# Layer norm in smaller groups, activation tables loaded early, copies out of PSUM shared with VectorE, loads and weight folds interleaved: a new prologue for a fused attention and FFN kernel

## The chip, the cores and the metric

The kernel runs on one core of a Trainium2 chip. The metric is the time of one execution in microseconds of device time. The profile's span is some 1.7 us shorter than that time (195.4 for a run of 197.16). Executions of this kernel fall into bands, and the result section tells them apart by span and mean granted TensorE clock. A run more than 1.5% above the fastest of its kernel counts as slow; all others are fast, and ratios use fast runs alone. In the profile, PE is TensorE, PEld its weight loads, DVE is VectorE, ACT is ScalarE and POOL is GpSimd. PSUM is the memory that TensorE writes; its results must be copied out to SBUF, the main on-chip memory.

## The reference

```python
def reference(A_x, A_wqkv, A_w_phi, A_wo, B_x, B_w1, B_w2):   # cut
    xn = layernorm(A_x)                       # [1, 2048, 448], no scale or bias
    q, k, v = split_heads(xn @ A_wqkv)        # 16 heads of 28
    pq, pk = q @ w_phi, k @ w_phi             # per head, 28 x 28
    phi = lambda p: concat(softmax(p), softmax(-p))
    kv = einsum("bhsf,bhsd->bhfd", phi(pk), v); z = phi(pk).sum(over s)
    o  = (phi(pq) @ kv) / (phi(pq) @ z + 1e-6)
    return A_x + o @ A_wo + silu(xn @ B_w1) @ B_w2          # hidden size 1792
```

The attention is linear, with sums over all tokens, so any assignment of tokens to tiles gives the same answer. `w_phi` can be multiplied into the q and k weights once, before the tokens are processed; this is called the fold below. `rstd` below is one over the standard deviation of a token, by which layer norm multiplies.

## The kernel before

A small scheduler collects operations with their reads and writes, adds the semaphore waits and emits them **in program order on each engine**. An engine that waits for one operation therefore does nothing else until it comes. The 2048 tokens are 16 tiles of 128.

```python
# prologue (order of emission; what each part runs on is noted)
def ln_stats(t):     # DVE: bn_stats, bn_aggr -> mean and variance of tile t
def ln_rstd(g, n):   # POOL: add eps, pow(-0.5), for n tiles at once
def ln_apply(t):     # DVE: xn = (x - mean) * rstd, bf16
def xn_transpose(t): # PE: four transposes into PSUM bank "tp"
def xnT_evac(t0):    # DVE: PSUM -> SBUF for a pair of tiles
def emit_wprep_transposes_r(r):   # PE: 8 weight transposes; ACT: copy out of PSUM
    tp_banks = [B_TP, B_PQ[0], B_PQ[1], B_TP]
    ...
def emit_wphi_chain():            # DVE: centre w_phi, block-diagonal form
def emit_wprep_fold():            # PE: wT x w_phi -> wk2, wq2; copies out of PSUM:
    ...                           # ACT, but DVE for q folds 1 and 3
def emit_kv_zero():               # DVE: clear PSUM banks 4, 5

LNG = 4; LA = 6
LF = LA + LNG - 1
for t in range(0, 4): ln_front(t)            # stats; rstd after tile 3
emit_wprep_transposes_r(2); emit_wprep_transposes_r(3)      # k weights
for t in range(0, 4): xn_make(t)             # apply, transpose, copy the pair
emit_wphi_chain(); late_loads()
emit_wprep_transposes_r(0); emit_wprep_transposes_r(1)      # q weights
for t in range(4, 8): ln_front(t)
emit_wprep_fold(); emit_kv_zero()
for t in range(4, LA): xn_make(t)
for t in range(8, LF): ln_front(t)

for t in range(NT):                          # the token loop
    if t + LF < NT: ln_front(t + LF)
    if t + LA < NT: ln_apply(t + LA)
    kv_proj(t); k_exps(t); v_evac(t); k_norm(t)   # PE; ACT; ACT; DVE, DVE, POOL
    q_block(t)                                    # PE, then two exps on ACT
    if t + LA < NT: ...                           # transpose, copy of a pair
    if t >= 1: kv_acc(t - 1)
kv_acc(NT - 1); rhs_build()
# then the long stretch: four FFN blocks, one attention tile, one output tile a round
```

The token loop looks six tiles ahead with normalisation and nine with statistics. x is loaded in four DMAs of four tiles, and each output tile is stored by a DMA of its own.

The softmax here doesn't subtract the row's maximum and nothing guards it: scores larger than these inputs give would overflow.

## Time and profile before

| | before |
|---|---|
| median, all its first 16 runs | 198.73 us (197.15 to 201.41) |
| profiled run | 197.16 us, span 195.4, mean clock 0.991 |
| first key projection | 22.02 us |
| long stretch of TensorE begins | 79.31 us |
| last output addition begins | 192.61 us |

A table of busy time by stretch divides the span. Its columns are the stretch, its length, busy time and instruction count of PE, PEld, DVE, ACT and POOL, then TensorE's granted clock, DMA share and GB/s. These rows cover the prologue, the loop and the long stretch of the kernel before:

```profile
0.00:22.00 22.00, 8.99 (x88) 8.30 (x89) 12.01 (x30) 7.34 (x11) 4.11 (x15) 1.00 0.76 215
22.00:75.00 53.00, 49.08 (x347) 28.92 (x345) 37.70 (x63) 38.57 (x78) 27.85 (x19) 0.97 0.13 38
75.00:178.00 103.00, 100.49 (x637) 51.44 (x636) 51.21 (x123) 43.26 (x67) 2.20 (x2) 1.00 0.04 13
```

Read each row by its fullest engine. In the prologue that is VectorE, busy 12.01 us although nothing reached it before 5.83. TensorE is the fullest engine in the two stretches after that. ScalarE has 14.7 free microseconds in the prologue.

### The profile page before, as it was taken

How to read it: one execution, taken by the hardware profiler on the slowest of the kernel's cores; microseconds unless marked ns; L12 is line 12 of the kernel's file. 1: busy time of each engine (PE TensorE's matmuls, PEld its weight loads, DVE VectorE, ACT ScalarE, POOL GpSimd, SP SyncE). 2: the span in 40 equal slices, each digit the busy share in tenths (PEclk: the TensorE clock that was granted, in tenths of full speed). 3: DMA queues.
4: the chain of work that ended last, by engine and by line, in shares of the span. 5: the costliest groups of instructions: out<-in, count | busy, mean ns of one | idle time of the engine just before them, and what ended most of it. 6: DMA issues, size and time to landing. Idle time of an engine off the chain costs nothing.

```text
span 195.4 us, 2897 instructions
## 1 busy us (share of the span) xinstructions
PE 173.1 (89%) x1152; PEld 96.4 (49%) x1152; DVE 106.7 (55%) x227; ACT 90.2 (46%) x156; POOL 34.2 (17%) x35
## 2 busy tenths in 40 slices
PE   0349696996999995899999999999999999999994
PEld 0338364553655553444545545545545545455551
DVE  0559895995775553377626336336345355288221
ACT  2307366676678888457343433433424424420200
POOL 3111136555556566000000000000000000000000
PEclk9999789999999999999999999999999999999999
DMA  5947980000000000000000000000000000000001
GB/s 159 306 163 196 293 254 1 0 2 5 0 0 3 0 0 2 3 0 0 0 27 0 23 23 0 29 23 0 23 29 0 23 23 3 23 18 29 26 24 47
DMA packets 9022, 8.70 MB, mean 45 GB/s; under 512 B 880, under 2 KB 8560, under 8 KB 9008
## 3 DMA queue, kind: packets, MB, share of 16 engines
q1 hardware_dynamic: 7616, 7.31, 12.7%
q10 hardware_dynamic: 1392, 1.20, 2.2%
q8 instruction: 9, 0.15, 0.3%
q14 instruction: 5, 0.04, 0.1%
HBM read 6.68 MB, written 1.84 MB: 44 GB/s over the span
## 4 chain that ended last, share of the span: by engine, by line
PE 69%; DVE 3%; POOLq 1%; issue 1%; ACT 1%
PE ps L553 25%; PE ps L634 22%; PE ps L637 6%; PE ps L570 3%; PE ps L443 3%; PE ps L510 3%; PE ps L451 2%; PE ps L495 2%; PE ps L612 2%; DVE xn_sb L409 1%; DVE S_sb L475 1%; POOLq L199 1%; ACT E_sb L461 1%; PE ps L422 1%; DVE R_sb L479 0%
## 5 line engine op out<-in xcount | busy, mean ns | idle before, releaser
L559 ACT ACTIVATE hT_sb<-ps 128x512 bf16<-128x512 f32 x56 | 33.4, 597 | 52.8 <-PE ps L553 52.8
L553 PE MATMUL ps<-xnT_sb,w_sb 112*128 112x512 bf16 x224 | 50.7, 379 | 0.0
L634 PE MATMUL ps<-w_sb,hT_sb 128*128 128x448 bf16 x224 | 45.0, 352 | 0.0
L553 PEld LDWEIGHTS ps<-xnT_sb,w_sb 112*128 112x128 bf16 x224 | 19.5, 98 | 27.2 <-ACT hT_sb L559 8.9
L481 POOL TENSOR_TENSOR phik_sb<-E_sb,R_sb 128x896 bf16<-128x896 f32 x16 | 27.6, 1724 | 28.1 <-DVE R_sb L479 23.9
L634 PEld LDWEIGHTS ps<-w_sb,hT_sb 128*128 128x128 bf16 x224 | 21.3, 98 | 17.9
L583 DVE RECIPROCAL rneg_sb<-ps 128x16 f32<-128x16 f32 x16 | 4.1, 256 | 38.1 <-PE ps L570 38.1
L475 DVE TENSOR_REDUCE S_sb<-E_sb 128x32 f32<-128x896 f32 x16 | 17.3, 1082 | 10.5 <-ACT E_sb L461 10.5
L646 DVE TENSOR_TENSOR y_sb<-ps,x_sb 128x448 bf16<-128x448 f32 x16 | 10.0, 625 | 16.9 <-PE ps L637 16.9
L518 ACT ACTIVATE EqT_sb<-ps 112x512 bf16<-112x512 f32 x32 | 17.4, 594 | 3.9 <-PE ps L510 3.9
L510 PE MATMUL ps<-xnT_sb,wq_sb 112*112 112x512 bf16 x64 | 17.0, 389 | 0.0
L422 PE MATMUL ps<-ident_sb,xn_sb 128*112 128x128 bf16 x64 | 7.1, 249 | 9.8 <-DVE xn_sb L409 9.5
L451 PE MATMUL ps<-wv_sb,xnT_sb 112*128 112x448 bf16 x64 | 15.5, 367 | 0.0
L443 PE MATMUL ps<-wk_sb,xnT_sb 112*128 112x448 bf16 x64 | 15.2, 360 | 0.0
L637 PE MATMUL ps<-wo_sb,EqT_sb 112*128 112x448 bf16 x64 | 14.8, 353 | 0.0
L458 ACT ACTIVATE E_sb<-ps 128x448 f32<-128x448 f32 x16 | 8.7, 544 | 12.0 <-PE ps L443 11.7
L409 DVE TENSOR_SCALAR xn_sb<-x_sb,mv_sb,rstd_sb 128x448 bf16<-128x448 bf16 x16 | 10.4, 667 | 5.3 <-POOL rstd_sb L402 5.3
L619 ACT ACTIVATE EqT_sb<-ps 112x1024 bf16<-112x1024 bf16 x8 | 8.2, 1024 | 11.0 <-PE ps L612 10.8
L391 DVE BATCH_NORM_STATS2 stats_sb<-x_sb 128x6 f32<-128x448 bf16 x16 | 9.6, 598 | 5.8 <-DMA x_sb<-in_A_x_dram 5.8
L422 PEld LDWEIGHTS ps<-ident_sb,xn_sb 128*112 128x112 bf16 x64 | 5.6, 149 | 13.9 <-DVE xn_sb L409 13.1
L495 PE MATMUL ps<-vaug_sb,phik_sb 128*112 128x113 bf16 x128 | 9.5, 215 | 2.5 <-POOL phik_sb L481 2.5
L510 PEld LDWEIGHTS ps<-xnT_sb,wq_sb 112*112 112x112 bf16 x64 | 8.7, 136 | 5.6 <-issue 0.8
(49 smaller groups left out, 159.7 us busy)
## 6 DMA issues: line engine op xcount, KB each, us to landing
w_sb<-in_B_w_dram SPq DMA_DIRECT2D x2, 1568.0 KB, 11.2
x_sb<-in_A_x_dram SPq DMA_DIRECT2D x4, 448.0 KB, 8.7
out_dram<-y_sb SPq DMA_DIRECT2D x16, 112.0 KB, 1.7
hT_sb<-in_A_wqkv_dram ACTq DMA_DIRECT2D x2, 392.0 KB, 6.2
wv_sb<-in_A_wqkv_dram ACTq DMA_DIRECT2D x1, 392.0 KB, 8.8
wo_sb<-in_A_wo_dram SPq DMA_DIRECT2D x1, 392.0 KB, 8.9
wphi_sb<-in_A_w_phi_dram SPq DMA_DIRECT2D x1, 24.5 KB, 5.4
```

What stands on the lines that cost most here:

```text
L422: last = e.transpose(out=bank_bf(B_TP)[0:KC, half * 512 + c * P: half * 512 + (c + 1) * P], in_=xn_sb[:, slot, c * KC:(c + 1) * KC], ident ...
L443: last = e.matmul(bank(B_PK[s2])[:, 0:D], lhsT=xnT_sb[:, c, t * P:(t + 1) * P], rhs=wk2_sb[:, c, :], start=(c == 0), stop=(c == NC_ - 1))
L451: last = e.matmul(bank(B_V)[:, 0:D], lhsT=xnT_sb[:, c, t * P:(t + 1) * P], rhs=wv_sb[:, c, :], start=(c == 0), stop=(c == NC_ - 1))
L475: sch.add("dve", lambda e: e.tensor_reduce(out=S_sb[:, s2, :], in_=E_sb[:, s2, :].rearrange("p (g f) -> p g f", f=DH), axis=AX.X, op=ALU.add),
L481: sch.add("pool", lambda e: e.tensor_tensor(out=phik_sb[:, s2, :].rearrange("p (g f) -> p g f", f=DH), in0=E_sb[:, s2, :].rearrange("p (g ...
L495: last = e.matmul(bank(B_KV[sg])[0:KC, j * NV:(j + 1) * NV], lhsT=phik_sb[:, s2, sg * D + j * KC: sg * D + (j + 1) * KC], rhs=vaug_sb[:, s ...
L510: last = e.matmul(bank(B_PQ[slot])[0:KC, :], lhsT=wq2_sb[:, c, j * KC:(j + 1) * KC], rhs=xnT_sb[:, c, tg * TG:(tg + 1) * TG], start=(c == ...
L518: sch.add("act", lambda e, sg=sg: e.activation(out=EqT_sb[:, j, sg, tg * TG:(tg + 1) * TG], in_=bank(B_PQ[slot])[0:KC, :], func=ACTF.Exp, ...
L553: last = e.matmul(bank(B_PQ[slot])[:, :], lhsT=w1_sb[:, c, k * P:(k + 1) * P], rhs=xnT_sb[:, c, tg * TG:(tg + 1) * TG], start=(c == 0), st ...
L559: sch.add("act", lambda e: e.activation(out=hT_sb[:, k, tg * TG:(tg + 1) * TG], in_=bank(B_PQ[slot])[:, :], func=ACTF.Silu), reads=["bank: ...
L634: last = e.matmul(bank(B_ACC[s2])[:, 0:D], lhsT=hT_sb[:, k, t * P:(t + 1) * P], rhs=w2_sb[:, k, :], start=(k == 0), stop=False)
L637: last = e.matmul(bank(B_ACC[s2])[:, 0:D], lhsT=oT_sb[:, c, t * P:(t + 1) * P], rhs=wo_sb[:, c, :], start=False, stop=(c == NC_ - 1))
```

## The change

The intent is to start normalisation after two tiles, not four, to hide ScalarE's table loads, to share PSUM copies between two engines, and to move x and y in longer runs. The diff, cut to its core:

```diff
-    x2 = A_x[0]
-    out2 = out[0]
+    x3 = A_x[0].rearrange("(p t) d -> p t d", t=NT)      # 3584 B runs a load
+    out3 = out[0].rearrange("(p t) d -> p t d", t=NT)
 ...                                                     # loads: wqk0 to the SP queue, x2 to the ACT queue
+        sch.add("act", ... activation(out=dummy_sb[:, 0:1], in_=epsln_sb[:, 0:1], func=ACTF.Sqrt) ...)
 ...  emit_wprep_transposes_r
-                if False:
+                if r % 2 == 1:                          # copy on DVE, else ACT
 ...  emit_wprep_fold -> emit_wprep_fold_qk(qk)
-                    if qk == 1 or i % 2 == 0:           # copy on ACT, else DVE
+                    if i % 2 == 0:
 ...  ln_rstd, path "act":
+                sch.add("act", ... veps = Sqrt(var + eps) ...)
+                sch.add("dve", ... rstd = reciprocal(veps) ...)
 ...  final_out: one store for two tiles
+            if t % 2 == 1:
+                dma("sp", out3[:, t0:t0 + 2, :], y_sb[:, s4 - 1:s4 + 1, :], ...)
 ...
+        groups = [(0, 2, "act"), (2, 4, "act"), (4, 8, "pool"), (8, 12, "pool"), (12, 16, "pool")]
 ...  prologue
+        ln_front(0); ln_front(1)
         emit_wprep_transposes_r(2); emit_wprep_transposes_r(3)
+        ln_apply(0); ln_apply(1); ln_front(2); ln_front(3)
+        ... activation(out=dummy_sb[:, 1:2], ..., func=ACTF.Exp)      # preload
         emit_wphi_chain()
+        xn_transpose(0); xn_transpose(1); xnT_evac(0)
+        emit_wprep_fold_qk(1)
+        ln_apply(2); ln_apply(3); xn_transpose(2); xn_transpose(3); xnT_evac(2)
         late_loads()
         emit_wprep_transposes_r(0); emit_wprep_transposes_r(1)
         for t in range(4, 8): ln_front(t)
+        emit_wprep_fold_qk(0)
         emit_kv_zero(); ...
 ...  loop: q_block(0) in iteration 1
```

## The prediction

> **What bounds the kernel now.** I read the page's slices first, then the chain of waits, then the order of work of VectorE before 23 us, because the change touches only the front of the kernel and its stores.
>
> Two rows of the slices of the page (each digit is the busy tenth of 4.9 us):
>
> ```profile
> PE   0349696996999995899999999999999999999994
> DVE  0559895995775553377626336336345355288221
> ```
>
> From the sixteenth slice on TensorE is full; in the first five it is not, and there VectorE (DVE) is the fuller engine. The chain that ended last says the same (start, length, what):
>
> ```profile
> 78.69 0.62 PE ps L495 x8
> 79.31 3.46 PE ps L553 x16
> ...
> 191.81 0.77 PE ps L637 x4
> 192.58 0.02 issue
> 192.61 0.62 DVE y_sb L646
> ```
>
> In it TensorE alone runs from 79.31 to 192.58 without a gap. So 113 us are matmuls that the change doesn't touch: the change can gain or lose only in the time until the first key projection (L443), in the token loop (to 79 us), and in the tail after the last matmul. The loop's start in TensorE's order of work (start, busy time):
>
> ```profile
> 21.45 0.73 PE L422 MATMUL ps<-ident_sb,xn_sb 128*112 128x128 bf16 x8 [2.01 <-DVE xn_sb L409]
> 22.02 1.37 PE L443 MATMUL ps<-wk_sb,xnT_sb 112*128 112x448 bf16 x4
> ```
>
> TensorE waited 2.01 us for VectorE to normalise tiles 4 and 5. VectorE's order of work up to there (lines of it, start, busy time, idle before and its releaser):
>
> ```profile
> 5.83 0.63 DVE L391 BATCH_NORM_STATS2 stats_sb<-x_sb 128x6 f32<-128x448 bf16 x1 [5.83 <-DMA x_sb<-in_A_x_dram]
> ...
> 10.33 0.70 DVE L409 TENSOR_SCALAR xn_sb<-x_sb,mv_sb,rstd_sb 128x448 bf16<-128x448 bf16 x2 [1.48 <-POOL rstd_sb L402]
> 11.92 0.69 DVE L432 COPY xnT_sb<-ps 112x1024 bf16<-112x1024 bf16 x1 [0.89 <-PE ps L422]
> 12.53 0.69 DVE L409 TENSOR_SCALAR xn_sb<-x_sb,mv_sb,rstd_sb 128x448 bf16<-128x448 bf16 x2
> 14.11 0.69 DVE L432 COPY xnT_sb<-ps 112x1024 bf16<-112x1024 bf16 x1 [0.89 <-PE ps L422]
> ...
> 18.93 1.17 DVE L382 CAST wq_sb<-ps 112x448 bf16<-112x448 f32 x2
> 20.31 0.91 DVE L387 MEMSET ps<- 128x1024 f32 x1 [0.21 <-ACT wq_sb L378]
> 21.13 0.56 DVE L409 TENSOR_SCALAR xn_sb<-x_sb,mv_sb,rstd_sb 128x448 bf16<-128x448 bf16 x2
> ```
>
> From 5.83 to 21.7 VectorE idles only 1.48+0.89+0.89+0.21 = 3.47 us. It is the prologue's bound: what is put onto it, or makes it wait, moves the loop's start. In the loop up to about 55 us it also paces: POOL's products start 3.34 us apart (38.20, 41.55, 44.89), while TensorE's share of a tile is 3.0 us.
>
> **What the Trainium skill says.** "ScalarE: Activation LUTs", section "What ACT_TABLE_LOAD costs": a load takes about 1283 ns and its drain 1380 ns; with a pointer bias an activation costs about 280 ns plus its elements; "Table sets: the hidden batching unit" adds that exp and sqrt lie in different sets, while copy is in every set. The trace agrees with the load (1.28 us at 2.42 and at 76.70) and with copy needing no second load before exp; the drain and sqrt it does not show. "DMA: Bandwidth & Descriptors", section "Queues, rings and completion order": each DMA engine alternates between queues by packets of several descriptors. So a queue with longer descriptors should get more of the engine (my inference); not visible in before, where both queues have 896 B runs. "TensorE: Matmul & The Clock Gate", part 1: matmuls after a few us of idleness run at half clock; the trace agrees (four key matmuls busy 1.37 us at 22.02, 0.92 us later). "SBUF — State Buffer", "Who interferes with whom": VectorE's fast modes and GpSimd lock each other out; the trace agrees (normalising a tile takes 264 ns at least, 1.34 us beside POOL's product at 35.34).
>
> **The change part by part.** Slots below are start-to-start times on VectorE from its order of work: statistics of a tile 0.73, normalisation 0.33, copy of a transposed pair 0.61, weight fold out of PSUM 0.59, phi weights 1.15 (14.71 to 15.86), memset 0.82.
>
> What VectorE loses: the wait for POOL's rstd (1.48). What it gains: two transposed-weight copies from ScalarE (estimate 0.53 each, the 0.61 scaled by 896/1024 elements), two more fold copies (0.59 each), two tiny reciprocals (estimate 0.15 each, from the 0.18 of the small ops). That is 2.5 us more work against 1.5 us of wait. ScalarE, which is relieved, was idle most of the prologue (7.34 busy of the first 22 us).
>
> But engines work in order, so the new order must be walked. The k weights land at 6.2 (TensorE's first transpose is at 6.22) and the 16 weight transposes take 1.75, so to 8.0. Statistics 0, 1 and their sqrt and reciprocal fit before that (5.83+1.46+0.5 = 7.8). VectorE then:
> - copy of transposed weights 3: 8.0 to 8.5; normalise 0, 1 to 9.2; statistics 2, 3 to 10.65; sqrt on ScalarE and reciprocal, about 0.5, to 11.15; phi weights to 12.3; copy of pair 0 to 12.9.
> - folds of k start only at 12.35, a fold takes 0.375 (32 matmul groups of four, 2.99 us for eight): fold 1 is done at 13.1, copied to 13.7; fold 3 at 13.85, copied to 14.45.
> - normalise 2, 3 to 15.1; their transposes end 1.55 after the first normalisation began (10.33 to 11.92 now), at 16.0; copy to 16.65. Idle 0.9.
> - The q weights' transposes use the same PSUM bank, so begin at 16.65 and take 1.71; copy 1 of them is now VectorE's, ahead of the next statistics: idle 1.7, copy 18.35 to 18.9. This is the worst new wait: before, the same transposes ran beside the statistics of tiles 4 to 7.
> - statistics 4 to 7 to 21.8; q fold copies to 23.0; memset to 23.8; normalise 4 starts 23.8 instead of 21.13.
>
> The first key projection follows 0.89 after it, as now: 24.7 instead of 22.02, **+2.7**. In short, from 8.0 on 12.5 us of slots and idle of 0.35 (sqrt), 0.2 and 0.15 (folds), 0.9, 1.7 = 3.3: as much idle as the old 3.47, and the added work comes on top.
>
> Table preloading: sqrt's load (1.28) follows ScalarE's DMA issues, ends about 4, hidden. The exp load after the second sqrt ends at about 12.4 (with a drain 13.7), before or about when the first k fold must be copied by ScalarE: not on the path. Gain 0: exp's load was never on the path (one load at 2.42, hidden).
>
> Query block 0 moved from iteration 0 to 1: same work. Before, VectorE waited 0.24 at 28.27 for the second key exponentials, which stood behind that block; this may go: **-0.25**. Groups 8 to 11 and 12 to 15 stay with POOL, so the stalls of 1.91 and 1.90 us for rstd at 32.94 and 47.94 stay. The VectorE/POOL cycle and the two stalls carry a late start through; I see no slack in which it is regained.
>
> Loads: x goes from runs of 896 B to 3584 B. x arrives sooner, but what starts the chain is the k weights at 6.2, which may lose bandwidth beside the longer runs of x and the q weights now third on the other queue: estimate **+0.2** (between -0.3 and +0.7; x0 plus k weights are 840 KB, 2.8 us at the 306 GB/s of the second slice). Later loads are needed long after landing.
>
> Stores: 16 of 112 KB become 8 of 224 KB. In the loop they are hidden. The last must now carry twice the bytes after the last addition (ends 193.23, span ends 195.4): 112 KB more at 306 GB/s is 0.37, less what longer runs save: **+0.3**.
>
> Sum 2.7-0.25+0.2+0.3 = 2.95, on 197.88: about **200.8 us**, 1.5% slower.
>
> **Rivals.** (1) The intended gain: the LN wait of 1.48 and the waits of 0.89 for transposes vanish behind other work, the loop starts near 19.5, 195.3 us. For it: those waits are truly on the path. Against: VectorE's added 2.5 us, and its in-order waits for folds and q transposes; even with no wait after 8.0 but the second sqrt's (0.35), VectorE's slots sum to 12.5 us and normalise 4 starts at 20.8, only 0.3 earlier than now; 195.3 would need 18.6. (2) Table thrash: if copies between the sqrts need their own set, each switch is 1.28 to 2.66 us and sits before the second sqrt, on VectorE's path: 202 to 204. Against: copy and exp share one load now. (3) The loss is hidden: the loop's first tiles run on a cold clock and with loose coupling, so a later but more complete start (q block later, warmer array) loses only 1 us: 199. For: 4.1 us were spent from 22.02 to 26.08 on the first tile. Against: VectorE's statistics and key sums, not TensorE, lead to the rstd stall at 31.0. (4) Late k weights: up to 1 us more, 201.8.
>
> **Range and chances.** Rival 3 and early weights give the lower end, 198.8; late weights and part of rival 2 the upper, 203.2. Two per cent slower is 201.84, 1 us above my centre: chance 0.23. Two per cent faster is 193.9 and would need the loop to start 4 us sooner, which the slot sum forbids: 0.03. Within 2%: 0.74.
>
> **What would show it.** In the changed profile: first key projection (L443's line moved) at 24 to 25.5 us; VectorE idle 1.5 us or more before the copy of the second q-weight half, waiting for TensorE; VectorE busy 2 us more before that; three table loads; stalls of 1.5 to 2 us for POOL's rstd in the loop still there; TensorE's gapless stretch starting 2 to 3 us later than 79.15; the time from the last addition to the end 0.2 to 0.4 longer. Wrong would be: k weights landing before 5.5, a first projection before 22, extra table loads, or the stalls in the loop shrinking.

## The result, and the profile after

The changed kernel took **202.48 us** (median of 11 runs, 200.64 to 204.41) against 198.73 before (16 runs). The ratio is 1.0179, with a 95% interval of 1.0133 to 1.0224, so it is about 1.8% slower and the interval lies on both sides of two per cent. Two of the 11 runs (203.68 and 204.41) were slow, and two of the 16 (200.50 and 201.41) lie as far above their fastest; the medians include them, the ratio does not. Here and below, a ratio is the mean time of one kernel's fast runs over that of the other's fast runs of the same rounds, so it is not quite the ratio of the medians.

These are the same two slice rows after the change, with the row of granted clock:

```profile
PE   0445399699699999699999999999999999999993
DVE  0674979699495455337564264264264264288321
PEclk9999999999999999799999999999999999999999
```

TensorE's full stretch starts a slice later. The 7 in the clock row at slice 17 is a second, smaller matter, taken up below.

VectorE's order of work in the changed kernel shows the waits (start, busy time, what, then the idle time before it and its releaser):

```profile
7.28 0.17 DVE L420 RECIPROCAL rstd_sb<-veps_sb 128x2 f32<-128x2 f32 x1 [0.36 <-ACT veps_sb L416]
8.34 0.62 DVE L356 COPY hT_sb<-ps 112x896 bf16<-112x896 bf16 x1 [0.90 <-PE ps L346]
...
11.42 0.17 DVE L420 RECIPROCAL rstd_sb<-veps_sb 128x2 f32<-128x2 f32 x1 [0.36 <-ACT veps_sb L416]
...
13.87 1.37 DVE L388 CAST wk_sb<-ps 112x448 bf16<-112x448 f32 x2 [0.55 <-PE ps L372]
...
16.74 0.69 DVE L449 COPY xnT_sb<-ps 112x1024 bf16<-112x1024 bf16 x1 [0.89 <-PE ps L439]
19.32 0.62 DVE L356 COPY hT_sb<-ps 112x896 bf16<-112x896 bf16 x1 [1.89 <-PE ps L346]
...
24.95 0.56 DVE L426 TENSOR_SCALAR xn_sb<-x_sb,mv_sb,rstd_sb 128x448 bf16<-128x448 bf16 x2
```

The wait of 1.48 for POOL's rstd is gone, and two waits of 0.36 for ScalarE's sqrt stand in its place. But two lines are new: copies of transposed weights (L356) now sit on VectorE, behind waits of 0.90 and 1.89 us for TensorE. Tile 4, which gates the loop, is normalised at 24.95 instead of 21.13.

TensorE's order of work shows where this leads:

```profile
25.27 1.10 PE L439 MATMUL ps<-ident_sb,xn_sb 128*112 128x128 bf16 x8 [3.46 <-DVE xn_sb L426]
26.16 1.70 PE L460 MATMUL ps<-wk_sb,xnT_sb 112*128 112x448 bf16 x4
...
37.41 0.43 PE L439 MATMUL ps<-ident_sb,xn_sb 128*112 128x128 bf16 x4 [1.76 <-DVE xn_sb L426]
...
82.36 0.65 PE L512 MATMUL ps<-vaug_sb,phik_sb 128*112 128x113 bf16 x8 [2.17 <-POOL phik_sb L498]
82.83 5.30 PE L570 MATMUL ps<-xnT_sb,w_sb 112*128 112x512 bf16 x16
```

TensorE waits 3.46 us for tile 4 (2.01 before), and the first key projection starts at 26.16. The delay then travels:

| start of | before | after | difference |
|---|---|---|---|
| normalise tile 4 | 21.13 | 24.95 | +3.82 |
| normalise tile 8 | 32.94 | 36.96 | +4.02 |
| normalise tile 12 | 47.94 | 51.96 | +4.02 |
| long stretch | 79.31 | 83.01 | +3.70 |
| second FFN round | 83.19 | 88.55 | +5.36 |
| last output addition | 192.61 | 197.97 | +5.36 |
| end of span | 195.4 | 201.0 | +5.6 |

There are three parts: 3.7 us from the prologue, 1.66 us in the first FFN round, and 0.24 us after the last addition. The 1.66 us are the slice with clock 7. The sixteen FFN matmuls of that round took 5.12 us in the chain, against 3.45 to 3.50 in every later round.

That part does not belong to the change alone. The changed kernel's ten fast runs whose spans are on record (one more than the median counts) have two bands: four from 198.9 to 199.2 at clock 1.0, and six from 200.7 to 201.5 at 0.983 to 0.992. The profiled run is of the longer band, while the profiled run of before is of that kernel's shortest. Shortest band against shortest band (198.9 against 195.3 us in the runs of the experiments) gives 3.6 us; the medians differ by 3.75.

### The profile page after: what moved, and what is told of

It is laid out like the page before. It is cut to its first block, busy times and chain, and to the rows that moved or that the text cites.

```text
span 201.0 us, 2883 instructions
## 1 busy us (share of the span) xinstructions
PE 175.4 (87%) x1152; PEld 97.1 (48%) x1152; DVE 109.3 (54%) x233; ACT 90.4 (45%) x157; POOL 32.9 (16%) x34
## 4 chain that ended last, share of the span: by engine, by line
PE 68%; DVE 3%; POOL 1%; issue 1%; ACT 1%; POOLq 0%
PE ps L570 25%; PE ps L651 21%; PE ps L654 6%; PE ps L587 3%; PE ps L460 3%; PE ps L527 3%; PE ps L468 2%; PE ps L512 2%; PE ps L629 2%; DVE xn_sb L426 1%; DVE S_sb L492 1%; POOL phik_sb L498 1%; ACT E_sb L478 1%; PE ps L439 1%; DVE R_sb L496 0%
## 5 line engine op out<-in xcount | busy, mean ns | idle before, releaser
L570 PE MATMUL ps<-xnT_sb,w_sb 112*128 112x512 bf16 x224 | 52.4, 388 | 0.0
L570 PEld LDWEIGHTS ps<-xnT_sb,w_sb 112*128 112x128 bf16 x224 | 20.0, 100 | 28.4 <-ACT hT_sb L576 8.6
L527 PE MATMUL ps<-xnT_sb,wq_sb 112*112 112x512 bf16 x64 | 16.3, 379 | 0.0
L468 PE MATMUL ps<-wv_sb,xnT_sb 112*128 112x448 bf16 x64 | 15.0, 358 | 0.0
```

The lines of the kernel that those rows point to most:

```text
L468: last = e.matmul(bank(B_V)[:, 0:D], lhsT=xnT_sb[:, c, t * P:(t + 1) * P], rhs=wv_sb[:, c, :], start=(c == 0), stop=(c == NC_ - 1))
L527: last = e.matmul(bank(B_PQ[slot])[0:KC, :], lhsT=wq2_sb[:, c, j * KC:(j + 1) * KC], rhs=xnT_sb[:, c, tg * TG:(tg + 1) * TG], start=(c == ...
L570: last = e.matmul(bank(B_PQ[slot])[:, :], lhsT=w1_sb[:, c, k * P:(k + 1) * P], rhs=xnT_sb[:, c, tg * TG:(tg + 1) * TG], start=(c == 0), st ...
```

## The experiments

Each kernel ran beside the kernel before on the same chip, six runs each except the last. All outputs are right. The ratio given is to that kernel's fast runs of the same rounds. One run each of experiments 2 and 5, and one of the kernel before in the second set, was slow and is in the median alone. The median of the kernel before was 198.21, 198.31 and 198.33 us in the three sets of rounds.

**The theory:** VectorE bounds the prologue, and its in-order copies and their waits move everything after it. **The rivals:** late weights, TensorE's clock, or the new order and the table loads themselves.

### 1. The transposed-weight copies back on ScalarE (changed kernel)

```diff
-                if r % 2 == 1:
+                if False:
```

> The changed kernel with the two transposed-weight copies given back to ScalarE, nothing else. Theory (VectorE's in-order work bounds the prologue): the two waits of VectorE for weight transposes (0.90 and 1.89 us) and the two copies (0.54 each) leave its path; normalise 4 starts near 21.7 instead of 24.95, the time falls by about 3.2 us from the changed kernel, to within 0.5 us of the kernel before. Rival (late k weights or TensorE's clock cause the loss): less than 1 us falls.

The median was 198.88 us, ratio 1.0037 (0.9992 to 1.0082); tile 4 was normalised at 21.85:

```profile
21.85 0.56 DVE L426 TENSOR_SCALAR xn_sb<-x_sb,mv_sb,rstd_sb 128x448 bf16<-128x448 bf16 x2
```

Undoing these **two copies takes back most of the loss**: 2.8 us by the ratios, and 2.8 by the shortest spans (196.1 against 198.9). The rivals are out as main causes: the loads, the order and the tables were still the changed kernel's, and the two bands, 1.7 us apart, were still there.

### 2. The same work in another order (changed kernel)

```diff
         emit_wprep_transposes_r(0)
+        ln_front(4); ln_front(5)
         emit_wprep_transposes_r(1)
-        for t in range(4, 8): ln_front(t)
+        ln_front(6); ln_front(7)
```

> The changed kernel with the same instructions, but VectorE takes the statistics of tiles 4 and 5 ahead of the second q-weight copy. Theory: of the 1.89 us wait about 1.45 is filled with work; normalise 4 starts near 23.3 instead of 24.95, the time falls 1.5 us. Rival (it is the amount of VectorE work that costs, the wait is only slack): less than 0.5 us falls.

The median was 200.13 us, ratio 1.0102 (1.0048 to 1.0156); tile 4 at 23.02. Nothing was taken from VectorE. The wait itself, filled with work that was due anyway, was worth 1.5 us by the ratios (1.0179 less 1.0102) and by the shortest spans (197.4 against 198.9). Tile 4 came 1.9 us earlier in the trace, but 0.47 of that is k weights that landed sooner (6.09 against 6.56).

### 3. Only the four copies moved (kernel before)

```diff
-                if False:
+                if r % 2 == 1:
-                    if qk == 1 or i % 2 == 0:
+                    if i % 2 == 0:
```

> The kernel before, with only the four PSUM copies (two transposed-weight, two k-fold) moved to VectorE. Theory: 2.2 us of VectorE work and about 0.8 of wait; normalise 4 at 23 to 23.5 instead of 21.13, the time rises by 2 to 2.5 us. Rival (ScalarE was the prologue's bound, the copies help): the time falls.

The median was 201.15 us, ratio 1.0150 (1.0108 to 1.0192); tile 4 at 23.48:

```profile
23.48 0.56 DVE L409 TENSOR_SCALAR xn_sb<-x_sb,mv_sb,rstd_sb 128x448 bf16<-128x448 bf16 x2
```

So **the copies alone make 3 us of loss in a kernel that has nothing else of the change**. Some 2.4 us of it is the later tile 4; the rest, in these two traces, is more of the first matmuls at half speed (their transposes took 1.10 us and the first key projection 1.70, against 0.73 and 1.37 before; the interval from tile 4 to tile 8 was 12.47 us against 11.81).

### 4. Only the layout: long runs of x, paired stores (kernel before)

The edit is the first two lines of the diff with the loads and the paired store that go with them.

> The kernel before, with only the token layout changed: x loaded in 3584 B runs and y stored in pairs. Theory: x arrives up to 0.5 us sooner, the last store costs 0.24 more: the time stays within 0.5 us. Rival (the long runs take bandwidth from the k weights): the first weight transpose starts at 6.6 or later and the time rises by 0.5 to 1.

The median was 197.88 us, ratio 0.9976 (0.9932 to 1.0020), the same within the interval. x arrived at 4.76 instead of 5.83, and the k weights at 5.93 instead of 6.22. The longer runs took nothing from the other queue (with the same loads in experiments 10 and 11 the k weights landed at 6.23 and 6.18), so that rival falls. With the changed kernel's own order of loads the k weights landed at 6.09 to 6.20 in four traces (experiments 1, 2, 7 and 8), as before (6.00 to 6.22 in five traces), but at 6.49 and 6.56 in two (experiment 6 and the changed kernel); there x was late as well (5.45 and 5.35, against 4.79 to 4.92). Why these two differ is open. The last addition began 0.88 us earlier in the profiled run, and the time from its end to the end of the span was 2.45 us against 2.17: the paired last store costs 0.28 us.

### 5. Only the layer norm part (kernel before)

```diff
-        for t in range(0, 4): ln_front(t)
-        emit_wprep_transposes_r(2); emit_wprep_transposes_r(3)
-        for t in range(0, 4): xn_make(t)
+        ln_front(0); ln_front(1)
+        emit_wprep_transposes_r(2); emit_wprep_transposes_r(3)
+        ln_apply(0); ln_apply(1); ln_front(2); ln_front(3)
+        # exp table preload; sqrt on ScalarE for tiles 0, 1 and 2, 3
+        xn_transpose(0); xn_transpose(1); xnT_evac(0)
+        for t in range(2, 4): xn_make(t)
```

> The kernel before, with only the layer norm part of the change: sqrt on ScalarE for tiles 0, 1 and 2, 3, tables preloaded, tiles 0 and 1 normalised before the statistics of 2 and 3; all PSUM copies stay where they were. Theory (the change's LN part is a gain that the copies swamp): of VectorE's waits the 1.48 for POOL goes and two of about 0.36 come; one of the 0.89 goes; normalise 4 at about 19.7 instead of 21.13, the time falls by 1 to 1.5 us. Rival (the split and the tables cost as much as they save): no fall.

The median was 195.92 us, ratio **0.9883** (0.9836 to 0.9931); tile 4 at 20.00. The idea of the change is a gain, also with sqrt and its tables on ScalarE. The traces give 1.1 us at tile 4 and 0.7 at the long stretch, and the profiled run was the longest of its fast runs. Their shortest span is 193.5 against 195.3 of before, that is 1.8 us. The ratio's 2.3 us thus includes a different mix of bands.

### 6. All four copies back on ScalarE (changed kernel)

This is experiment 1 and, for the folds, `if qk == 1 or i % 2 == 0`.

> The changed kernel with all four moved PSUM copies (two transposed-weight, two k-fold) back on ScalarE. Theory: beside the 3.1 us of the weight copies another 1.2 to 1.7 us leave VectorE's path (1.29 of k-fold copies and their wait of 0.55, less a new wait for transposes); normalise 4 at 20.3 to 20.7, the time 1 us under that with the weight copies alone back, some 0.5 us under the kernel before. Rival (the new order itself costs): it stays above the kernel before.

The median was 198.36 us, ratio 1.0000 (0.9948 to 1.0053). By the ratio this missed: the time equals that of the kernel before. Tile 4 came at 21.18, not before 20.7, but that is the loads: x landed at 5.45, against 4.87 in experiment 1, and VectorE carries these 0.58 us through to the copy of the first pair (11.36 against 10.77). Less 0.58, tile 4 is at 20.6, as expected, and the shortest span (195.0) is 1.1 us under that of experiment 1, also as expected. VectorE's order of work in this run shows two long waits:

```profile
14.13 0.69 DVE L449 COPY xnT_sb<-ps 112x1024 bf16<-112x1024 bf16 x1 [1.48 <-PE ps L439]
...
18.77 1.37 DVE L388 CAST wq_sb<-ps 112x448 bf16<-112x448 f32 x2 [1.03 <-PE ps L372]
```

The transposes of tiles 2 and 3 now stand behind the k folds on TensorE, so VectorE waits 1.48 instead of 0.89, and 1.03 for the q folds (this one stood in experiment 1 too). Experiment 5, without the new order, has a shortest span of 193.5, 1.5 us less than here. That the new order costs what the layer norm part gains is likely from these waits, but not shown: the two kernels differ in their loads, their stores and the q block too.

### 7. FFN blocks into TensorE's idle time, first try (changed kernel)

```diff
+        ffn1_block(0); ffn1_block(1)
         kv_acc(NT - 1)
-        nf = 0
+        nf = 2
```

> The changed kernel with the first two FFN blocks ahead of the last key-value product, so that TensorE has no idle of 2.2 us before its long stretch. Theory (TensorE's clock falls in a window that holds this idle time, in some runs): the first FFN groups run at full clock in every run, the runs no longer split into two bands 1.7 us apart, and the time falls 1.7 us (two blocks of 0.86 moved into the idle) beside it: all runs near 199 us. Rival (the low-clock window comes at a fixed place whatever TensorE does): the two bands stay 1.7 us apart.

The median was 209.21 us, ratio 1.0564 (1.0520 to 1.0607): a plain miss. The chain of waits shows why (start, length, what):

```profile
94.70 0.02 issue
94.73 1.03 ACT EqT_sb L636
95.76 0.05 issue
95.81 2.82 PE ps L651 x14
```

The condition that starts the output products came true one round earlier, so each pair of them stood directly behind ScalarE's copy of the transposed attention output, which it reads. TensorE waited 1.12 us before them in every second round, 8.9 us in all. The six runs were all at a clock of 0.999 or 1.0, but this kernel is too different to judge the bands by.

### 8. The same with the old distance (changed kernel)

```diff
-            if t < NT and nf >= (t // TPG + 1) * NK and no > (t | 1):
+            if t < NT and nf >= min((t // TPG + 1) * NK + 2, NTG * NK) and no > (t | 1):
```

> The run with two FFN blocks ahead of the last key-value product again, with its fault mended: there the output products began one round earlier, straight behind the copies of the transposed attention output (TensorE waited 1.3 us in every second round). Here they keep their old distance. Theory (the idle before the long stretch brings the low-clock window into the FFN): all runs in one band at full clock, near a span of 197.3 (199.0 of the changed kernel's full-clock runs less 1.7), so 3 us under the changed kernel's median. Rival (the window is at a fixed place): two bands 1.7 apart remain, the lower at 197.3.

The median was 198.87 us, ratio 1.0040 (1.0010 to 1.0070). All six spans lay between 197.1 and 197.4: **one band**. TensorE's order of work at the place in question:

```profile
79.56 1.89 PE L570 MATMUL ps<-xnT_sb,w_sb 112*128 112x512 bf16 x8
81.89 0.62 PE L512 MATMUL ps<-vaug_sb,phik_sb 128*112 128x113 bf16 x8 [0.44 <-POOL phik_sb L498]
82.35 3.62 PE L570 MATMUL ps<-xnT_sb,w_sb 112*128 112x512 bf16 x16
```

The idle time fell from 2.17 to 0.44, and the first full FFN round took 3.62 us of busy time, not 5.30. The changed kernel had the longer band in six of its ten fast runs; here none of six has it, and experiments 7 and 11, which fill the same idle time, ran at a clock of 0.998 to 1.0 in all twelve runs. So a window at a fixed place, whatever TensorE does, is very unlikely. The idle time is a condition for the long round, but not enough for it: with 2.17 to 2.53 us of idle time five traces have it (4.88 to 5.14 us) and six have not (3.46). What decides between them is open.

### 9. Statistics one iteration earlier (kernel before)

```diff
-        LF = LA + LNG - 1
+        LF = LA + LNG
```

> The kernel before, with the statistics of every tile from 9 on one iteration earlier, so that POOL's rstd of tiles 8 to 11 and 12 to 15 is asked for an iteration ahead of its use. Theory (the loop's start is carried through because VectorE waits for POOL twice): the waits of 1.91 and 1.90 us vanish, the FFN starts 2.5 to 3.8 us earlier. Rival (the loop is paced by the 3.34 us cycle of VectorE and POOL, the waits are its slack): under 1 us.

The median was 195.76 us, ratio 0.9875 (0.9836 to 0.9913). Both waits for POOL's rstd vanished: tile 12 was normalised at 43.99, against 47.86 in the repeated kernel before (experiment 12). But the long stretch began only 2.67 us earlier (76.57 against 79.24). The other 1.2 us of the 3.87 were probably slack: after tile 12 came the part of the loop where TensorE is busy without a gap (from 54.94 to 73.96 in the kernel before's chain).

### 10. A prologue made by the theory

From the kernel before, with other PSUM banks for the q folds too: x in long runs, the layer norm part, all copies as they were, phi weights and statistics of tile 4 where VectorE would wait, the q weights' transposes in PSUM banks 7 and 6 instead of the shared one, and the last two stores single.

```diff
+            tp_banks = [B_PQ[1], B_PQ[0], B_PQ[1], B_PQ[0]]
 ...
+        xn_transpose(0); xn_transpose(1); emit_wphi_chain(); xnT_evac(0)
+        ln_apply(2); ln_apply(3); xn_transpose(2); xn_transpose(3)
+        ln_front(4); xnT_evac(2); late_loads()
+        emit_wprep_fold_qk(1)
+        emit_wprep_transposes_r(0); emit_wprep_transposes_r(1)
+        for t in range(5, 8): ln_front(t)
+        emit_kv_zero(); ln_apply(4); ln_apply(5)
+        emit_wprep_fold_qk(0); xn_transpose(4); xn_transpose(5); xnT_evac(4)
```

> A prologue made by the theory: the kernel before with x in long runs, the LN split, all copies as before, phi weights and statistics put where VectorE would wait, the q weights' transposes in banks of their own, the last two stores single. Theory: normalise 4 starts near 17 instead of 21.13, limited by POOL's rstd of tiles 4 to 7, the first key projection near 19, and the time falls by 2.5 to 3.5 us from the kernel before, to about 195. Rival (the loop takes the gain back in its waits for POOL): under 1.5 us falls.

The median was **193.41 us**, ratio 0.9795 (0.9739 to 0.9851), some 4 us better than before. Tile 4 was normalised at 17.46, the first key projection began at 18.49 and the long stretch at 75.55. This beats the expectation, with the same mechanism: VectorE's listed waits up to tile 4 sum to 1.28 us, against 3.47 before. Four of the six runs had a span of 191.6 or 191.7, two were longer (193.2 and 194.1 at a clock of 0.99).

```profile
17.46 0.70 DVE L425 TENSOR_SCALAR xn_sb<-x_sb,mv_sb,rstd_sb 128x448 bf16<-128x448 bf16 x2 [0.35 <-POOL rstd_sb L410]
```

### 11. All three together

Experiment 10 with the edits of 9, 7 and 8.

> The prologue made by the theory, with the statistics one iteration earlier and two FFN blocks ahead of the last key-value product at the old distance of the output products. Theory: the gains add: 193.4 less 2.5 to 3.5 (loop waits) less 1.7 (idle): 188 to 189.5 us. Rival (the loop is paced by VectorE and POOL): 191 to 192.

The median was **190.36 us**, ratio 0.9613 (0.9578 to 0.9647). It beats both kernels in every run (spans 188.1 to 189.1). The gains do not quite add: 3.05 us under experiment 10 by the medians, where 4.2 to 5.2 were expected. Tile 12 came 3.68 us earlier than there, but only about 1.8 us of it reached the end of the last key-value product; in experiment 9 too, part of the gain was lost on the way. Between the two profiled runs, both at a clock of 1.0, the difference is 3.6 us.

### 12. The kernel before once more

> The kernel before once more, for its trace in another clock band: its runs had spans of 195.3 to 195.6 at a mean clock of 0.991 and 196.5 to 197.3 at 1.0 or 0.983. Theory: in the longer band the extra 1 to 1.5 us lie in the first tiles of the loop or in the first FFN group at half clock, not in VectorE's order up to normalise 4, which stays at 21.1. Rival: the prologue itself is longer (weights or x land later).

This run took 198.76 us, span 197.0, mean clock 0.983. It lies among the kernel's fast runs of that set (197.05 to 198.82). Tile 4 was normalised at 20.95, as early as ever, and the long stretch began at 79.24. The clock row and the first FFN round of this trace:

```profile
PEclk9999699999999999699999999999999999999999
...
79.08 5.30 PE L553 MATMUL ps<-xnT_sb,w_sb 112*128 112x512 bf16 x16
```

So the kernel before also has the slow first FFN round in some of its runs, and here it is the whole difference to its first profiled run (5.14 less 3.46 us, spans 197.0 and 195.4). What stays open: other runs of before have spans of 196.4 to 197.3 with a recorded clock of 1.0, and no trace fell on one of them. Their extra microsecond is not located.

## Why the prediction was right

The prediction said 200.8 us and slower by 1.5%; 202.48 and 1.8% came, inside its range. The difference was to be 2.95 us; it was 3.6 by the shortest bands and 3.75 by the medians. The term that was too small is the 2.7 us for the loop's start: tile 4 was normalised 3.8 us later and the long stretch began 3.7 us later. Two of the prediction's signs were overshot with it: the first key projection came at 26.16, not 24 to 25.5, and the long stretch 3.7 us later, not 2 to 3. The other signs came, and none of those of being wrong. One reading of the page was off: the sixteenth slice of TensorE's row is a 5, and the engine is full from the seventeenth on (8, then 9). Its steps, against the changed kernel's trace:

| step of the walk along VectorE | predicted | measured |
|---|---|---|
| k weights there | 6.2 | 6.56 |
| copy of transposed weights 3 | 8.0 | 8.34 |
| phi weights done | 12.3 | 12.64 |
| normalise 2 | 14.45 | 15.16 |
| copy of tiles 2, 3 | 16.0 | 16.74 |
| wait for q-weight transposes | 1.7 | 1.89 |
| statistics 4 | 18.9 | 19.86 |
| normalise 4 | 23.8 | 24.95 |
| first key projection | 24.7 | 26.16 |
| last store, extra | +0.3 | +0.24 |

- **The bound.** Right. Experiments 1 and 3 show it from both sides: taking the two weight copies off VectorE gains 2.8 us, and putting all four copies onto it costs 3.0. The traces of experiments 7 and 8, which leave this part of the changed kernel alone, repeat the delay: tile 4 at 24.59 and 24.49. Experiment 2 shows that the worst new wait was the one named.
- **The sizes.** The walk was 1.15 us short at normalise 4. About 0.35 is k weights that landed later in this trace, the separate +0.2 of the sum; in four of six traces with the same loads they came at 6.09 to 6.20, so it is variation between runs. Another 0.35 to 0.4 is the k folds: they began about 0.2 us later after the phi weights than I allowed, and sixteen matmuls took 1.72 us, not the 1.5 that I scaled from a longer burst. The rest is another hand-off of about 0.2 and a wait that I left out. I let TensorE begin the q-weight transposes when VectorE's *slot* ended, but it began after the copy's full duration and a little more (the copy at 16.74 ended at 17.43; the transposes began at 17.57). And VectorE is idle for 0.21 us before it clears PSUM, just ahead of tile 4, in both kernels.
- **The loop.** Right that nothing is regained: tile 8 is as late as tile 4, and both waits for POOL (1.92 and 1.90) are still there. The term of -0.25 was about -0.1: from tile 4 to the long stretch the changed kernel took 58.06 us against 58.18.
- **Tables.** Right: three loads, none on the path. The exp load lies at 11.41 to 12.69, before ScalarE's first fold copy at 13.49.
- **The rivals.** The intended gain exists (experiment 5), but in this kernel the copies swamp it. Table thrash did not come. Rival 3, a loss partly hidden in the first tiles, did not come: they ran at half clock here too, and tile 8 was 0.2 us later still. Late k weights came in two of six traces, by some 0.3 us.
- **Not foreseen.** TensorE's half-clock window in the first FFN round, worth 1.66 us in runs of either kernel. It is the main reason why a profiled run shows +5.6 where the shortest bands differ by 3.6; the rest is of the size of that run's late k weights. I had not read the runs of before for bands, and the range held partly by luck on this point.

## What to carry to other kernels

Before sharing work between engines, ask which engine sets the end of *that stage* and what stands behind the moved instruction in its order. A copy moved to an engine brings the wait for its producer with it, and on an in-order engine everything behind pays for both. Here 14.7 us of idle time on ScalarE made room for four copies that VectorE could not afford. When the wait can't be removed, put work in front of it that is due anyway; that alone was worth 1.5 us in experiment 2. And read the spans of all runs for bands before comparing two profiles: one pair of traces here differed by 2 us more than the kernels did.

## What the Trainium skill lacked or had wrong

- "ScalarE: Activation LUTs", section "What ACT_TABLE_LOAD costs", adds a drain of about 1380 ns to each load. In the changed kernel's trace the activation began at 3.60 after a load from 2.31 of 1.28, and at 12.70 after one from 11.41 of 1.28: no such gap, 1.29 us for each switch. The load's figure and the sqrt with a pointer bias (0.30 us for two columns) agree.
- "TensorE: Matmul & The Clock Gate", part 1, gives an idle window of about 3.4 us before the clock falls. Here a longest idle time of 2.2 to 2.5 us came before a slow round in five traces: the next sixteen matmuls took 4.88 to 5.14 us instead of 3.46. With the same idle time six traces show no slow round. Filled to 0.44 us, it came in none of six runs.
- The same page warns that clock events are unreliable; the runs add a case. In experiment 5 the recorded clock was 1.00 from 22 to 26 us while four matmuls took 1.70 us that took 0.92 later. The length of a known matmul group is the better witness.
- "DMA: Bandwidth & Descriptors", section "Queues, rings and completion order", gives arbitration by packet, but not what longer runs in one queue do to the other; I inferred that they delay it. In the trace of experiment 4 they did not: with runs of 3584 B instead of 896 B, x landed at 4.76 instead of 5.83 and the k weights of the other queue at 5.93 instead of 6.22; with the same loads in experiments 10 and 11 these came at 6.23 and 6.18.
